# Row sums of an attention pair: written to DRAM as nine rows after one transpose, instead of element by element

## The chip, the cores and the metric

The kernel runs on one core of a Trainium2 chip. The metric is the device time of one execution in microseconds; the median of three runs of the kernel before is 1294.0 us (1293.81 to 1294.35). Engines are named as in the profile: PE (TensorE; PEld its weight loads), DVE (VectorE), ACT (ScalarE), POOL (GpSimd) and SP (SyncE), which issues every DMA of this program on one queue, in program order.

## The reference

```
q_pool = q.reshape(2, 8, 576, 2, 64).mean(axis=3)        # pairs of queries averaged
scores = q_pool @ k.T / 8 ; scores -= max(scores)         # 576 x 1152 for each of 16 heads
attn   = exp(scores); attn /= attn.sum(-1) + 1e-9
x      = (attn @ v), heads side by side                   # 1152 tokens x 512
h = x @ w_in; x = (h * tanh(softplus(h))) @ w_out         # 512 -> 2048 -> 512
P = 8 rounds of Sinkhorn on exp(x @ w_gate - max)         # 1152 x 8 gates
out = sum over 8 experts of P[:, e] * (relu(x @ w1[e]) @ w2[e])
```

All values are float32; the kernel keeps each operand as a high and a low part and multiplies them in several passes. What is changed lies in the attention, at the division by the row sums `attn.sum(-1) + 1e-9`.

## The kernel before, in words

**Attention.** Two heads form a pair (8 pairs). The 2 x 576 query rows of a pair make nine tiles of 128 rows, numbered t = 0 to 8; tile 4 holds the end of one head and the start of the other, and so needs twelve score matmuls where the others need six. The loop at L678 has one step for each tile g = 9p + t and is a software pipeline. In program order a step does:

- `loads`: what an earlier step has put off, all of it DMAs, issued on SP (L685 to L687);
- `scores(g)`: six (tile 4: twelve) matmuls into `psS` (L453), and on DVE the negated copy to `e` with the row minimum (L458);
- `transposes(g - 3)`: nine PE transposes of the exponentials `er` (L527), evacuated by ACT as `eth` (L530) and by DVE as `etl` (L533);
- `hand_over(g - 1)`: a DMA that copies `e` of the tile before to `er` (L478), to be transposed two steps later;
- attention times values, `psA` (L548), in portions set by the table `AV`, and transposes of the next keys and queries, `psk` and `psq`;
- `exps(g)`: the exponential on ACT in place in `e` (L472), which also leaves the row sums of the tile in one column of `rs`, a tile of 128 x 9.

There are three buffers of `e` and two of `er`. Queries that have been transposed are copied to the other half of the partitions by small DMAs (`swap`, L426, tiles `qT` and `qz`); tile 4 needs `qz`.

**Row sums.** When pair p - 1 is complete, in the step t = 0 of pair p, `row_sums` (L480) adds EPS, takes the reciprocal on DVE (L482, L483) and puts two things on `loads`. `out` (L488) writes the 128 x 9 reciprocals into a DRAM tile `row`, transposed by its access pattern: each element goes to its own place, 1152 elements of 4 bytes. `back` (L493), one step later, reads `row` twice, spread over 64 partitions each, into `rx`. `back` waits until `row` has landed. `rx` is used by POOL once in each pair (L571), after the last `psA` of the pair.

**After the attention.** From step g = 73 on, `mish_step` starts the first layer of the next stage (L224, `ph`), which reads `xh` and `xl`, made by POOL after L571; weights come by `raw` DMAs (L139). From there to the end PE works through that stage (L224, L767) and the experts (L1028, L1186).

Of the kernel before, what the change touches and what calls it, by code (L numbers as in the profile page):

```python
# [8 lines left out]
F32 = mybir.dt.float32  # L9
# [14 lines left out]
def pool_attention_mish_sinkhorn_kernel(  # L24
# [12 lines left out]
    nc = tc.nc  # L37
    P = 128
    B, H, S, D = q.shape
    SQ = S // 2  # L40
# [6 lines left out]
    NPAIR = B * H // 2  # L47
    HPB = H // 2
    QTL = 2 * SQ // P
# [15 lines left out]
    ident = const.tile([P, P], F32, name="ident")  # L65
# [39 lines left out]
    def run(t, eng, most=99):  # L105

        q = queue[eng]
        while q and q[0][0] <= t and most > 0:
            q.pop(0)[1]()
            most -= 1  # L110
# [180 lines left out]
    with ExitStack() as actx:  # L291
        def pool(name, bufs, **kw):
            return actx.enter_context(tc.tile_pool(name=name, bufs=bufs, **kw))
# [20 lines left out]
        rx_p = pool("rx", 1)  # L314
        row_p = pool("row", 2, space=bass.MemoryType.DRAM)
# [5 lines left out]
        for i in range(2):  # L321
            t = z_p.tile([P, 2, 2, P], F32R, name=f"qz{i}")
# [4 lines left out]
        loads = []  # L327
# [20 lines left out]
        def split_kv(p, j, which, eng, part, more=True):  # L348
            if p == NPAIR:
                return  # L350
            raw = raws[which, p, j]
            pl, dst = (kst_p, kst) if which == "k" else (vst_p, vst)
            if part == 0:
                t = dst[p, j] = pl.tile([P, NK, 2, D], F32R, tag=which + "st", name=f"{which}st{p}_{j}")
                split_hi(eng, t[:, :, 0, :], raw)
            else:
                t = dst[p, j]
                split_lo(eng, t[:, :, 1, :], raw, t[:, :, 0, :])
                p, j = (p, 1) if j == 0 else (p + 1, 0)
                if more and p < NPAIR:  # L360
                    loads.append(lambda: load_kv(p, j, which))
# [79 lines left out]
        scS, eS, erS, rsS, rxS = {}, {}, {}, {}, {}  # L441

        def scores(g, pl=None):
            p, t = divmod(g, QTL)
            ps = (pl or ps_s).tile([P, 3, 512], F32, tag="s", name=f"psS{g}")
            for kb in range(3):
                if t == MID:
                    ops = [(qz[p % 2][:, j, s, :], kT[p, j]) for j in range(2) for s in range(2)]
                else:
                    x, i = q_tile(p, t)  # L450
                    ops = [(x[:, i, s, :], kT[p, int(t > MID)]) for s in range(2)]
                for n, (a, kt) in enumerate(ops):
                    nc.tensor.matmul(  # L453
                        ps[:, kb, 0:TH], lhsT=a, rhs=kt[:, kb * TH:(kb + 1) * TH],
                        start=(n == 0), stop=(n == len(ops) - 1))
            sc = e_p.tile([P, 3, TH], F32, tag="e", name=f"e{g}")
            nm = tiny.tile([P, 1], F32, tag="nm", name=f"nm{g}")
            nc.vector.tensor_scalar(  # L458
                sc, ps[:, :, 0:TH], -1.0, None, op0=ALU.mult, op1=ALU.min, accum_out=nm)
            scS[g] = (sc, nm)  # L460

        def exps(g):
            p, t = divmod(g, QTL)
            sc, nm = scS.pop(g)
            sc = sc.rearrange("p a b -> p (a b)")
            if g < 2:
                e = erS[g] = er_p.tile([P, S], F32, tag="er", name=f"er{g}")
            else:
                e = eS[g] = sc
            if t == 0:  # L470
                rsS[p] = tiny.tile([P, QTL], F32, tag="rs", name=f"rs{p}", bufs=2)
            nc.scalar.activation(e, sc, AF.Exp, bias=nm, scale=-1.0, accum_out=rsS[p][:, t:t + 1])  # L472

        def hand_over(g):

            e = eS.pop(g)
            er = erS[g] = er_p.tile([P, S], F32R, tag="er", name=f"er{g}")
            nc.sync.dma_start(out=er.bitcast(F32), in_=e)  # L478

        def row_sums(p):  # L480
            rs = rsS.pop(p)
            nc.vector.tensor_scalar(rs, rs, EPS, None, op0=ALU.add)  # L482
            nc.vector.reciprocal(rs, rs)  # L483
            row = row_p.tile([QTL * P], F32, tag="row", name=f"row{p}")
            rx = rxS[p] = rx_p.tile([P, SQ], F32, tag="rx", name=f"rx{p}")

            def out():
                nc.sync.dma_start(out=row.rearrange("(t p) -> p t", p=P), in_=rs)  # L488
                loads.append(back)

            def back():
                for j in range(2):
                    nc.sync.dma_start(  # L493
                        out=rx[j * D:(j + 1) * D, :], in_=row[j * SQ:(j + 1) * SQ].unsqueeze(0).to_broadcast([D, SQ]))

            loads.append(out)


        c0, c1 = 2 * P, SQ
# [80 lines left out]
        def run_av(n):  # L580
            for _ in range(n):
                if av_todo:
                    av_todo.pop(0)()
# [31 lines left out]
        ps_t = bctx.enter_context(tc.tile_pool(name="ps_w", bufs=2, space=PSUM))  # L615
# [38 lines left out]
        def prep(p, t):  # L654
            for x, at_ in (PREP if p else PREP0).items():
                if at_ == t:
                    if x[0] == "q":
                        split_q(p + 1, nc.gpsimd, int(x[1]))
                    else:
                        split_kv(p + (x[0] == "k"), int(x[1]), x[0], nc.gpsimd, int(x[2]))  # L660

        def turn(p, t):
            fs = []
            for j in range(2):
                pp = p + (j == 0)
                if pp < NPAIR:
                    fs += [
                        lambda pp=pp, j=j, c=c: trans_k(pp, j, c)
                        for c in range(3) if TURN["k10" if p == 0 and j == 1 else f"k{j}"][c] == t]
            for u in range(3):  # L670
                pp = p + (u == 0)
                if p == 0 and TURN["q0"][u] == t:
                    fs.append(lambda u=u: trans_q0(u + 2))
                if 0 < pp < NPAIR and TURN["q"][u] == t:
                    fs.append(lambda pp=pp, u=u: trans_q(pp, u))
            return fs

        for g in range(T0 + EARLY):  # L678
            p, t = divmod(g, QTL)
            if g == 1:  # L680
                bctx.close()
                ps_t = pool("ps_t", 4, space=PSUM)
                ps_a = pool("ps_a", 1, space=PSUM)
            pre = turn(p, t) if g < NQ else []
            waiting, loads[:] = loads[:], []  # L685
            for f in waiting:
                f()  # L687
            if g < LAG:
                exps(g)
                for f in pre:  # L690
                    f()
                if g + 1 < LAG:
                    split_kv(0, 0, "v", nc.gpsimd, g)
                    scores(g + 2, ps_s)
            else:
                if LAG < g < NQ:
                    scores(g)
                if p and g < NQ:
                    prep(p, t)
                if g < T0:  # L700
                    run(g, "dve")
                if pre:
                    pre.pop(0)()
                spread = 0 < p < NPAIR
                if spread:
                    run_av(AV[t][0])
                ready = len(av_todo)
                if g < NQ + LAG:
                    transposes(g - LAG)
                if g <= NQ:  # L710
                    hand_over(g - 1)
                if not p:
                    prep(p, t)
                run_av(min(ready, AV[t][1] if spread else 9 if g < NQ else 18))
                for f in pre:
                    f()
                if g < NQ:
                    exps(g)
            if p and t == 0:
                row_sums(p - 1)  # L720
            if late:
                late.pop(0)()
            if g < T0:
                run_all(g)
            if g == QTL:
                load_gate()
            if g == NQ - 1:
                sctx.close()
                ps_o = ctx.enter_context(tc.tile_pool(name="ps_o", bufs=3, space=PSUM, side="right"))
                wpools["d0"] = ctx.enter_context(tc.tile_pool(name="wd0", bufs=1, side="right"))  # L730
                mctx = ExitStack()
                wpools["d1"] = mctx.enter_context(tc.tile_pool(name="wd1", bufs=1, side="right"))
                wpools["t"] = mctx.enter_context(tc.tile_pool(name="wt2", bufs=3, side="right"))
            if g >= T0:
                mish_step(g - T0)
# [546 lines left out]
```

## Time and profile before

| | us |
|---|---|
| median of three runs | 1294.0 |
| the profiled execution's own time | 1296.31 |
| its span, first to last instruction | 1294.5 |

| engine | busy, us | share of the span |
|---|---|---|
| PE | 1233.8 | 95% |
| DVE | 853.2 | 66% |
| POOL | 622.1 | 48% |
| ACT | 596.6 | 46% |

The shares are means over stages that differ. In the page's forty slices the attention is the first ten; there DVE is at six to seven tenths, ACT at five to seven, PE at seven to nine, and the DMA engines at six to eight. In the later slices PE is at nine tenths or more and the DMA engines at one or two. The clock that was granted to PE is at 0.88 in the attention after the first pair and at 1.00 in the stages that follow. A wait is read from the timeline and the table of waits: how long an engine was idle, and whose end released it.

### The profile page before, as it was taken

The page shows a single profiled execution, that of the slowest core. Times are in us where ns is not written, and L with a number is a line of the kernel's source. Part 1 is how long each engine was busy: PE and PEld are TensorE (multiplying, and loading weights), DVE is VectorE, ACT ScalarE, POOL GpSimd, SP SyncE. Part 2 cuts the span into 40 slices and gives each one's busy share as a digit, 9 for nine tenths or more (in the row PEclk, how much of TensorE's full clock was granted, in tenths as well). Part 3 has the DMA queues.
Part 4 walks back from the last instruction along what each step waited for, and adds up shares of the span by engine and source line. Part 5 has one row for each costly group of instructions (what it writes and reads, how often), then busy time and mean ns, then how long its engine had stood idle before and what let it go on. Part 6 is the DMA issues. An engine that isn't in the chain of part 4 may idle for free.

```text
span 1294.5 us, 19313 instructions
## 1 busy us (share of the span) xinstructions
PE 1233.8 (95%) x6832; PEld 1134.3 (88%) x6832; DVE 853.2 (66%) x1580; ACT 596.6 (46%) x1364; POOL 622.1 (48%) x704
## 2 busy tenths in 40 slices
PE   8889787897999999999999999999999999999999
PEld 8779777787999999999888888889989998888887
DVE  7677666776464443368786666866776666866865
ACT  7677666775665454345233333333333333333331
POOL 5345524532253433327575555555555555555552
PEclk9889888988999999999999999999999999999999
DMA  6878888866432222001011111111111111111111
GB/s 207 196 191 224 241 193 173 199 224 159 130 112 82 82 82 62 13 17 50 26 45 38 49 49 49 50 42 49 50 49 50 49 50 49 31 40 42 45 49 73
DMA packets 76751, 116.84 MB, mean 90 GB/s; under 512 B 16496, under 2 KB 49008, under 8 KB 76656
## 3 DMA queue, kind: packets, MB, share of 16 engines
q1 hardware_dynamic: 76656, 115.62, 32.3%
q8 instruction: 54, 0.88, 0.3%
q14 instruction: 41, 0.34, 0.1%
HBM read 66.86 MB, written 2.40 MB: 54 GB/s over the span
## 4 chain that ended last, share of the span: by engine, by line
PE 81%; DMA 10%; DVE 6%; ACT 2%; issue 1%; SPq 1%; POOL 0%; ACTq 0%; DVEq 0%; POOLq 0%
PE po L1186 29%; PE c L1028 24%; PE ph L224 8%; PE po L767 7%; DMA er<-e 7%; PE psS L453 5%; DVE e L458 3%; PE psA L548 2%; DVE etl L533 2%; PE psT L527 1%; DMA qz<-qz 1%; DMA raw<-in_moe_w_in_dram 1%; DMA row<-rs 1%; ACT eth L530 1%; DVE xs L562 0%
## 5 line engine op out<-in xcount | busy, mean ns | idle before, releaser
L81 POOL TENSOR_TENSOR wslotsl<-s,wslotsh 128x256 fp32r<-128x256 f32 x180 | 132.3, 743 | 238.3 <-ACT wslotsh L74 227.2
L1194 DVE SCALAR_TENSOR_TENSOR oacc<-po,Pm,oacc 128x512 f32<-128x512 f32 (+1 forms) x217 | 161.2, 747 | 102.8 <-PE po L1186 95.4
L1186 PE MATMUL po<-wdbl,hhall 128*128 128x512 f32 (+1 forms) x543 | 214.6, 395 | 0.0
L1186 PE MATMUL po<-wdbh,hlall 128*128 128x512 f32 (+1 forms) x543 | 214.2, 395 | 0.0
L1186 PE MATMUL po<-wdbh,hhall 128*128 128x512 f32 (+1 forms) x543 | 214.2, 394 | 0.0
L458 DVE TENSOR_SCALAR_CACHE_REDUCE e<-psS 128x1152 f32<-128x1152 f32 x72 | 97.4, 1353 | 91.1 <-PE psS L453 46.0
L1045 ACT ACTIVATE t<-c 128x384 f32<-128x384 f32 x80 | 39.2, 490 | 247.1 <-PE c L1028 247.1
L1065 ACT ACTIVATE hhall<-c 128x384 fp32r<-128x384 f32 x180 | 88.5, 492 | 129.0 <-DVE c L1061 126.3
L1186 PEld LDWEIGHTS po<-wdbh,hhall 128*128 128x128 f32 x543 | 102.1, 188 | 24.3
L1186 PEld LDWEIGHTS po<-wdbl,hhall 128*128 128x128 f32 x543 | 102.1, 188 | 23.3
L1186 PEld LDWEIGHTS po<-wdbh,hlall 128*128 128x128 f32 x543 | 102.1, 188 | 23.2
L530 ACT ACTIVATE eth<-psT 128x384 fp32r<-128x384 f32 (+1 forms) x240 | 92.6, 477 | 57.1 <-PE psT L527 56.6
L81 POOL TENSOR_TENSOR wslotsl<-rawu,wslotsh 128x256 fp32r<-128x256 f32 x120 | 91.6, 777 | 51.5 <-ACT wslotsh L74 51.5
L533 DVE TENSOR_TENSOR etl<-psT,eth 128x384 fp32r<-128x384 f32 (+1 forms) x240 | 108.2, 508 | 5.6 <-ACT eth L530 4.4
L1066 DVE SCALAR_TENSOR_TENSOR hlall<-c,hhall 128x384 fp32r<-128x384 f32 x180 | 98.9, 549 | 2.1
L527 PE MATMUL psT<-identr,er 128*128 128x128 f32 x630 | 69.4, 256 | 32.3 <-DMA er<-e 31.0
L548 PE MATMUL psA<-etl,vst 128*128 128x256 f32 (+1 forms) x288 | 88.9, 326 | 9.0 <-DVE xs L562 8.5
L527 PEld LDWEIGHTS psT<-identr,er 128*128 128x128 f32 x630 | 63.4, 145 | 37.3 <-issue 32.9
L1028 PE MATMUL c<-x2h,wslotsl 128*128 128x384 f32 x280 | 94.8, 339 | 0.0
L1028 PE MATMUL c<-x2h,wslotsh 128*128 128x384 f32 x280 | 94.5, 338 | 0.0
L1028 PE MATMUL c<-x2l,wslotsh 128*128 128x384 f32 x280 | 94.2, 336 | 0.0
L472 ACT ACTIVATE e<-e,nm 128x1152 f32<-128x1152 f32 x70 | 89.0, 1271 | 0.9 <-ACT eth L530 0.8
(355 smaller groups left out, 3108.5 us busy)
## 6 DMA issues: line engine op xcount, KB each, us to landing
er<-e SPq DMA_DIRECT2D x70, 576.0 KB, 4.1
rawd<-in_moe_w_dram SPq DMA_DIRECT2D x60, 256.0 KB, 2.7
rawu<-in_moe_w_dram SPq DMA_DIRECT2D x30, 384.0 KB, 3.2
raw<-in_moe_w_in_dram SPq DMA_DIRECT2D x16, 512.0 KB, 3.9
raw<-in_moe_w_out_dram SPq DMA_DIRECT2D x16, 512.0 KB, 3.7
vraw<-in_v_dram SPq DMA_DIRECT2D x16, 288.0 KB, 3.9
kraw<-in_k_dram SPq DMA_DIRECT2D x15, 288.0 KB, 4.2
qraw<-in_q_dram SPq DMA_DIRECT2D x7, 576.0 KB, 6.8
```

Of the source, the lines that this page charges most:

```text
L81: eng.tensor_tensor(out=lo, in0=src, in1=hi.bitcast(F32), op=ALU.subtract)
L224: nc.tensor.matmul(ps[:, 0:TH], lhsT=a, rhs=b, start=(n == 0), stop=(n == len(ops) - 1))
L458: nc.vector.tensor_scalar(sc, ps[:, :, 0:TH], -1.0, None, op0=ALU.mult, op1=ALU.min, accum_out=nm)
L527: nc.tensor.transpose(pt[:, i, :], e[:, c * P:(c + 1) * P], ident if g < 2 else identr)
L530: nc.scalar.activation(eh[:, cs, o:o + b - a], ps[:, 0:3, a:b], AF.Copy)
L533: nc.vector.tensor_tensor(out=el[:, cs, o:o + b - a], in0=ps[:, 0:3, a:b], in1=eh[:, cs, o:o + b - a].bitcast(F32), op=ALU.subtract)
L548: nc.tensor.matmul(box["ps"][:, 0:n], lhsT=vst[p, j][:, c].rearrange("p a d -> p (a d)"), rhs=(el, eh)[which][:, c, 0:n], start=(c == 0 an ...
L767: nc.tensor.matmul(ps[:, 0:TH], lhsT=a, rhs=b, start=(n == 0), stop=(n == len(ops) - 1))
L1028: nc.tensor.matmul(cb[c], lhsT=a_, rhs=b_, start=FIRST[n] and m == 0, stop=LAST[n] and m == len(ops) - 1, skip_group_check=True)
L1066: los.append(lambda: nc.vector.scalar_tensor_tensor(out=lo, in0=b, scalar=0.0, in1=hi.bitcast(F32), op0=ALU.max, op1=ALU.subtract))
L1186: nc.tensor.matmul(ps[:, 0:w], lhsT=a, rhs=b[:, cs], start=(n == 0), stop=(n == len(ops) - 1))
L1194: nc.vector.scalar_tensor_tensor(out=oa, in0=ps[:, 0:w], scalar=gate, in1=oa, op0=ALU.mult, op1=ALU.add)
```

## The change

`row_sums` keeps the addition and the reciprocal. A new function, `turn_sums`, is called one step later (t = 1). It turns the 128 x 9 reciprocals into 9 x 128 by one PE transpose into a PSUM tile of the pool that `psT`, `psk` and `psq` use, copies them on DVE to an SBUF tile `rt`, and puts the write on `loads`. The DRAM tile `row` is now 9 x 128, and each of its rows is written from one partition of `rt` as 512 contiguous bytes. For all pairs but the last the write is put off by one step more, so that it is issued at the start of step t = 3 and the reads into `rx` at the start of t = 4; for the last pair they are issued at the start of the second and third step after the pair's end.

```
         def row_sums(p):
-            rs = rsS.pop(p)
+            rs = rsS[p]
             nc.vector.tensor_scalar(rs, rs, EPS, None, op0=ALU.add)
             nc.vector.reciprocal(rs, rs)
-            row = row_p.tile([QTL * P], F32, tag="row", name=f"row{p}")
+
+        def turn_sums(p):
+
+            ps = ps_t.tile([P, 4, P], F32, tag="t", name=f"psr{p}")
+            nc.tensor.transpose(ps[0:QTL, 0, :], rsS.pop(p), ident)
+            rt = rx_p.tile([QTL, P], F32, tag="rt", name=f"rt{p}")
+            nc.vector.tensor_copy(rt, ps[0:QTL, 0, :])
+            row = row_p.tile([QTL, P], F32, tag="row", name=f"row{p}")
             rx = rxS[p] = rx_p.tile([P, SQ], F32, tag="rx", name=f"rx{p}")
 
             def out():
-                nc.sync.dma_start(out=row.rearrange("(t p) -> p t", p=P), in_=rs)
+                nc.sync.dma_start(out=row, in_=rt)
                 loads.append(back)
 
             def back():
+                flat = row.rearrange("t p -> (t p)")
                 for j in range(2):
                     nc.sync.dma_start(
-                        out=rx[j * D:(j + 1) * D, :], in_=row[j * SQ:(j + 1) * SQ].unsqueeze(0).to_broadcast([D, SQ]))
-
-            loads.append(out)
+                        out=rx[j * D:(j + 1) * D, :], in_=flat[j * SQ:(j + 1) * SQ].unsqueeze(0).to_broadcast([D, SQ]))
+
+            loads.append(out if p == NPAIR - 1 else lambda: loads.append(out))
...
             if p and t == 0:
                 row_sums(p - 1)
+            if p and t == 1:
+                turn_sums(p - 1)
```

On SP, around the end of the third pair, the order before is this (`er` are the hand-overs, `qT` and `qz` the swapped queries, `vraw` and `raw` loads from DRAM):

```order
L478 DMA er_1619<-e_1551 128x1152
L488 DMA row_1637<-rs_1133 128x9x1
L478 DMA er_1683<-e_1596 128x1152
L493 DMA rx_1638<-row_1637 64x576 x2
L426 DMA qT_1_1655<-qT_1_1655 64x4x128 x2
L426 DMA qz_137<-qz_137 64x2x128 x2
L478 DMA er_1738<-e_1647 128x1152
L337 DMA vraw_1_1753<-in_v_dram 128x576
```

The same place of the changed kernel:

```order
L478 DMA er_1627<-e_1559 128x1152
L478 DMA er_1688<-e_1604 128x1152
L426 DMA qT_1_1660<-qT_1_1660 64x4x128 x2
L426 DMA qz_137<-qz_137 64x2x128 x2
L478 DMA er_1747<-e_1652 128x1152
L495 DMA row_1704<-rt_1702 9x128
L337 DMA vraw_1_1763<-in_v_dram 128x576
L426 DMA qT_2_1758<-qT_2_1758 64x128 x2
L478 DMA er_1812<-e_1717 128x1152
L139 DMA raw_0_2_1828<-in_moe_w_in_dram 128x512
L501 DMA rx_1705<-row_1704 64x576 x2
L478 DMA er_1868<-e_1774 128x1152
```

The write has moved behind one more hand-over and the swaps, and four other entries (five DMAs) now stand between it and the reads, where one hand-over stood.

On DVE at the same place the changed kernel has this order (`wt` are pieces of the weight preparation):

```order
L483 RECIPROCAL rs_1137<-rs_1137 128x9
L458 TENSOR_SCALAR e_1652,nm_1653<-psS_1645 128x1152
L162 SCALAR_TENSOR_TENSOR wt_0_1_1607<-raw_0_1_1324,wt_0_1_1607 128x256
L541 TENSOR_TENSOR etl_3_1669<-psT_0_1670,eth_3_1668 128x3x128
L541 TENSOR_TENSOR etl_3_1669<-psT_1_1676,eth_3_1668 128x3x128
L541 TENSOR_TENSOR etl_3_1669<-psT_2_1682,eth_3_1668 128x3x128
L490 COPY rt_1702<-psr_1700 9x128
L458 TENSOR_SCALAR e_1717,nm_1718<-psS_1710 128x1152
```

The copy L490 is the only new instruction there; it stands between the last `etl` of one step and the score copy of the next. On PE the transpose L488 stands at the same place, between the last `psA` of step t = 1 and the six `psS` matmuls of t = 2.

At the end of the last pair the order on SP before is:

```order
L139 DMA raw_0_2_4078<-in_moe_w_out_dram 128x512
L488 DMA row_4076<-rs_3620 128x9x1
L493 DMA rx_4077<-row_4076 64x576 x2
L139 DMA raw_1_0_4177<-in_moe_w_in_dram 128x512
L139 DMA raw_0_3_4179<-in_moe_w_out_dram 128x512
```

In the changed kernel it is:

```order
L139 DMA raw_0_2_4104<-in_moe_w_out_dram 128x512
L495 DMA row_4152<-rt_4150 9x128
L139 DMA raw_1_0_4207<-in_moe_w_in_dram 128x512
L139 DMA raw_0_3_4209<-in_moe_w_out_dram 128x512
L501 DMA rx_4153<-row_4152 64x576 x2
```

Two weight loads have moved ahead of the reads into `rx`.

## Rows read from the trace of the kernel before

**Rows 1.** The page's chain that ended last, by line.

```profile
PE po L1186 29%; PE c L1028 24%; PE ph L224 8%; PE po L767 7%; DMA er<-e 7%; PE psS L453 5%; DVE e L458 3%; PE psA L548 2%; DVE etl L533 2%; PE psT L527 1%; DMA qz<-qz 1%; DMA raw<-in_moe_w_in_dram 1%; DMA row<-rs 1%; ACT eth L530 1%; DVE xs L562 0%
```

**Rows 2.** Busy time by stage: the attention from its second pair; the passage after it.

```profile
core 0: us, PE busy (x) PEld busy (x) DVE busy (x) ACT busy (x) POOL busy (x), PEclk, DMA share, GB/s
...
38.00:328.50 290.50, 240.04 (x1665) 225.04 (x1664) 198.05 (x404) 200.24 (x448) 120.54 (x117) 0.88 0.78 199
328.50:359.00 30.50, 28.54 (x173) 27.60 (x174) 13.94 (x26) 18.85 (x39) 8.16 (x7) 1.00 0.40 114
```

**Rows 3.** Timeline of SP: start, duration of the issue, line, tiles.

```profile
121.52 0.39 SPq L488 DMA_DIRECT2D row<-rs  x1
122.07 0.49 SPq L478 DMA_DIRECT2D er<-e  x1
133.40 1.12 SPq L493 DMA_DIRECT2D rx<-row  x2
...
136.00 1.24 SPq L426 DMA_DIRECT2D qz<-qz  x2
137.33 0.56 SPq L478 DMA_DIRECT2D er<-e  x1
```

**Rows 4.** DMA issues of the whole span: count, KB each, median us to landing.

```profile
er<-e SPq DMA_DIRECT2D x70, 576.0 KB, 4.1
...
qraw<-in_q_dram SPq DMA_DIRECT2D x7, 576.0 KB, 6.8
...
out_dram<-oacc SPq DMA_DIRECT2D x2, 128.0 KB, 1.7
row<-rs SPq DMA_DIRECT2D x8, 4.5 KB, 10.1
```

**Rows 5.** DMA traffic from 121 to 134 us.

```profile
DMA packets 1319, 0.62 MB, mean 48 GB/s; under 512 B 1185, under 2 KB 1185, under 8 KB 1319
...
er<-e SPq DMA_DIRECT2D x1, 576.0 KB, 11.9
```

**Rows 6.** Waits of the DMA queue: total us, times, longest.

```profile
SPq L493 <- DMA row<-rs: 74.1, 8, 10.8
```

**Rows 7.** Timeline of DVE and PE, same place: start, duration, [idle before <- releaser].

```profile
124.39 1.35 DVE L458 TENSOR_SCALAR_CACHE_REDUCE e<-psS 128x1152 f32<-128x1152 f32 x1
...
134.04 1.36 DVE L458 TENSOR_SCALAR_CACHE_REDUCE e<-psS 128x1152 f32<-128x1152 f32 x1 [6.69 <-DMA er<-e]
134.06 1.35 PE L527 MATMUL psT<-identr,er 128*128 128x128 f32 x9 [5.70 <-DMA er<-e]
...
141.46 1.36 DVE L458 TENSOR_SCALAR_CACHE_REDUCE e<-psS 128x1152 f32<-128x1152 f32 x1 [3.69 <-PE psS L453]
```

**Rows 8.** Seven windows, L458 of tile 2 to L458 of tile 4, summed.

```profile
sum 124.00, PE 79.62 PEld 72.78 DVE 45.90 ACT 49.42 POOL 32.79; mean PE 11.37 PEld 10.40 DVE 6.56 ACT 7.06 POOL 4.68
```

**Rows 9.** Six windows, L458 of tile 4 to L458 of the next tile 2, summed.

```profile
sum 144.70, PE 139.82 PEld 132.76 DVE 132.04 ACT 131.72 POOL 82.82; mean PE 23.30 PEld 22.13 DVE 22.01 ACT 21.95 POOL 13.80
```

**Rows 10.** Busy time just after the wait of rows 7, and later in that pair.

```profile
134.00:138.50 4.50, 3.54 (x20) 3.38 (x20) 3.68 (x7) 1.25 (x3) 0.00 (x0) 0.50 0.58 153
138.50:145.00 6.50, 6.31 (x41) 5.74 (x41) 3.23 (x6) 4.80 (x9) 0.67 (x1) 0.91 0.90 272
145.00:154.00 9.00, 8.09 (x69) 7.59 (x69) 6.23 (x12) 7.42 (x16) 7.30 (x7) 1.00 1.02 350
```

**Rows 11.** Pieces of the chain of waits: start, us, what.

```profile
119.31 1.04 PE psS L453 x6
...
328.58 9.45 DMA row<-rs
```

**Rows 12.** The dearest like operations: a float32 PE transpose; a DVE read of PSUM.

```profile
L527 PE MATMUL psT<-ident,er x18: 272/273/331, 15.4 to 20.0; 128*128 128x128 f32 x18
...
L533 DVE TENSOR_TENSOR etl<-psT,eth 128x384 fp32r<-128x384 f32 (+1 forms) x240 | 108.2, 508 | 5.6 <-ACT eth L530 4.4
```

**Rows 13.** Timeline of PE after the attention: the longest wait there.

```profile
348.14 0.45 PE L224 MATMUL ph<-xl,wuh 128*128 128x384 f32 x1 [1.06 <-POOL xl L81]
```

## What is predicted, and how it is worked out

> **What bounds the kernel now.** I read the chain of waits first [rows 1]. Most of it is PE work of the later stages, which this change doesn't touch. What is not PE work and stands high is the hand-over DMA `er<-e`, 7% of the span, in a kernel whose hand-overs are meant to be hidden by the two steps between copy and use. The busy times by stage say where to look: from 38 to 328.5 us, in which 63 tiles run, PE is idle for 290.5 - 240.0 = 50.5 us, and its granted clock is 0.88; in the passage behind it PE is idle for 2.0 us at a clock of 1.00 [rows 2]. So a gain can come from those 290.5 us, and hardly from elsewhere.
>
> Next the queue's own timeline, around one pair's end [rows 3]. The element-wise `row` write is issued at 121.52, the next hand-over 0.55 us later, and then SP issues nothing until 133.40, when `row` has landed and the reads into `rx` may go. Everything behind them in the queue is late by that much: the swaps of `qz` go out at 136.00, the following hand-over at 137.33. In total SP stands at this wait for 74.1 us in eight pairs [rows 6]. The hand-over just behind the write is slow too: it lands 11.9 us after its issue, against a median of 4.1 us; in that stretch the DMA engines moved 1319 packets, 1185 of them under 512 bytes, and 1152 of these are the elements of `row` [rows 4, 5].
>
> The engines feel both halves [rows 7]. DVE copies the scores of tile 2 at 124.39; for tile 3 it waits 6.69 us for the hand-over to free its buffer, and PE waits 5.70 us to transpose the same tile; tile 4 then comes only at 141.46, since `qz` and the next hand-over were issued late. After the wait PE runs for a while at a granted clock of 0.50, the lower of its two levels (1.2 GHz), and is back at 1.00 only later in the pair [rows 10].
>
> **What the two late tiles are worth.** I cut the pairs at the score copies. From tile 2 to tile 4, two intervals, seven times: 124.0 us together, 17.7 each, with DVE busy for 6.6, ACT for 7.1 and PE for 11.4 of it, PE partly at the low clock [rows 8]. From tile 4 to the next pair's tile 2, seven intervals, six times: 144.7 us, or 144.7 / 42 = 3.45 per tile, with PE busy for 139.8, and DVE and ACT for 132 (91%) [rows 9]. That is the pace of this pipeline when no `row` write is in its way, near the limit of three engines. If tiles 3 and 4 ran at it, they would take 2 x 3.45, and 1.04 more for the six extra matmuls of tile 4 [rows 11], in all 7.93. Seven times 7.93 is 55.5. The most that the change can return here is therefore 124.0 - 55.5 = 68.5 us. At pair 3 the parts would be 6.2 of 9.65 us in the first interval and 2.9 of 7.42 in the second [rows 7].
>
> **The change, part by part.**
>
> Removed: the 1152 elements in each pair, so that the hand-over no longer waits behind them, and the wait of SP between write and reads. Gain as above, 68.5. What is late next in place of the 11.9 us hand-over is PE itself: with the hand-over landing 4.1 us after 122.07, at 126.2, PE would reach its transposes with the data there.
>
> Added: eight PE transposes of 9 x 128 and eight DVE copies. Neither shape is in the trace. A float32 transpose of 128 x 128 takes 0.27 us, a DVE read of three times as many columns from PSUM 0.51, so a third of it, 0.17, is my estimate for the copy [rows 12]. Below nothing neither can go. Two engines at 91% and 97% cover no such work, so I count both in full. The PSUM tile also shifts which of the four buffers the following transposes get, by one; the next `psT` then waits for the copy rather than for an older reader, some tenths at most. I take 0.5 us in each of seven pairs for all of it (0.2 to 0.9), 3.5 us. The copy holds up only the score copy behind it in DVE's queue.
>
> Moved: the write goes behind two hand-overs and two pairs of swaps, the reads behind one more hand-over, a pair of swaps and two loads. SP's own time for issues doesn't change, 0.4 to 0.6 us for each DMA. POOL's use of `rx` comes after the last `psA` of the pair, in step 5, more than one step behind the reads in either order.
>
> Crowding: today the loads and hand-overs held up by `row` go out together and fill the DMA engines, 350 GB/s at a share of 1.02 [rows 10]. From 134 to 154 us 5.6 MB moved (4.5 x 153, 6.5 x 272, 9 x 350), 16 us at that rate. With the wait gone the same tiles start at 125 and end some 9 us earlier, which leaves 20 us. So the engines are enough, but a hand-over may meet queries and weights. It has 6.9 us (two tiles) from issue to use and needs 4.1; the worst median of its size is 6.8 [rows 4]. I take 1.2 us lost in each pair, half as much again as PE's idle time in the good stretches (4.9 / 6 = 0.8), with bounds of 0 and 2.7 (6.8 - 4.1): 8.4 us.
>
> After the last pair the chain goes through the `row` write for 9.45 us [rows 11]. PE had other work beside it, and waits at most 1.06 us, for `xl` [rows 13]. `row` is issued one step later than now but lands faster, and two weight loads go ahead of the reads; I take 1.0 us of gain (0 to 1.4).
>
> **Sum.** 68.5 - 3.5 - 8.4 + 1.0 = 57.6 us. The profiled execution took 1296.3, 1.8 more than its span and 2.3 more than the median of the runs. It would become 1238.7, and the median 1294.0 - 57.6 = 1236.4, so I forecast 1236. With every bound on the good side the gain is 68.5 - 1.4 + 1.4 = 68.5, 1225.5; with every one on the bad side 68.5 - 6.3 - 18.9 = 43.3, 1250.7.
>
> **Rivals.**
>
> *The wait moves to the reads.* They still wait for `row`, and the hand-over of tile 3 is behind them. The nine rows may land in 1.7 us, as the small stores to DRAM at the end do, or, if they queue behind the hand-over issued just before, in up to 4.1 + 1.7 = 5.8 [rows 4]. SP comes to the reads about one tile, 3.45 us, later, so it stands there for 0 to 2.4 us. In the sum this is nothing, since the hand-over has 2.8 us to spare; if crowding has used that up, it is 2.4 us in seven pairs, 17 us: 1253. The Trainium skill (DMA: Bandwidth & Descriptors, Queues, rings and completion order) says that each DMA engine takes the descriptors of a ring in order. The trace agrees: the hand-over behind the elements took 11.9 us [rows 5]. By that rule the new write can't overtake the hand-over ahead of it, which is the upper end here.
>
> *Tile 4 still waits.* `qz` comes by two swaps that now follow the hand-over and may land too late. Then only the first interval is mended, and pair 3's 2.9 us stays in seven pairs: 20 us, 1257. Against it: behind the hand-over of 122.07 and one other pair of swaps (1.24 us a pair) they would be issued at about 124 instead of 136.00 [rows 3], and tile 4's matmuls are due at 124.39 + 7.93 - 2 x 1.04 = 130.2.
>
> *The write is as slow as before.* If nine rows of 512 bytes from nine partitions take as long as the elements, the order alone is changed. The time then lies at no gain and the new work, 1294.0 + 3.5 = 1297. The packets counted [rows 5] speak against it, since nine take the place of 1152.
>
> *Slower.* One mechanism: the write lands so late that SP is held at the reads for longer than now, with hand-over, queries and keys behind it. SP is held for 74.1 / 8 = 9.3 us today [rows 6]; with 3.45 us between the two this begins at a landing of 12.7 us. The element-wise write took 133.40 - 121.52 = 11.9 us beside a hand-over [rows 3]. At 15 us it would cost 2.3 us in seven pairs and the new work: 1294.0 + 16 + 3.5 = 1314. Nothing in the trace suggests it for nine packets.
>
> **Chances.** Forecast, with its own range of 1225 to 1251: 0.74. A wait moved to the reads: 0.10. Tile 4 still late: 0.09. Faster than 1225, because the long stretches also gain from free DMA engines: 0.03. Write as slow as before: 0.02. Slower by the held queue: 0.02. The range that should hold the time 8 times in 10 is 1224 to 1254; it takes in the first rival. A measurement of this kernel tells 0.2%, 2.6 us, from no change. Faster: 0.74 + 0.10 + 0.09 + 0.03 = 0.96; the same 0.01; slower 0.03, the last two cases shared.
>
> **What would show it.** In the changed profile the two-tile stretches should take about 9 us instead of 17.7, the seven-tile ones still about 24; the clock of the attention should be near 1.00; no hand-over should take more than about 7 us; SP's wait for `row` should be under 2.4 us in a pair; packets under 512 bytes should fall by some 9200; the time from the end of the attention to the end of the program should be as now. I am wrong if PE or DVE still waits for hand-overs in tiles 3 and 4, if tile 4 waits for `qz`, or if the long stretches grow by what the short ones lose.

## The result and the profile after

The changed kernel takes 1234.83 us (median of 4 runs, 1234.14 to 1235.62), the kernel before in the same runs 1294.17. The ratio is 0.954, with a 95% interval of 0.9524 to 0.9557. The forecast was 1236, the range 1224 to 1254. The profiled execution took 1235.16 us, with a span of 1233.3: 61.2 less than before. By the medians the gain is 59.3, where 57.6 was forecast.

The first view is the chain that ended last, by line, as in [rows 1]:

```profile
PE po L1196 30%; PE c L1038 26%; PE ph L224 10%; PE po L777 8%; PE psS L453 5%; PE psA L556 5%; DVE e L458 3%; PE psT L535 2%; DVE etl L541 2%; DVE xs L570 1%; ACT e L472 1%; ACT eth L538 1%; PE psk L391 1%; PE pg L832 0%; ACT kT L392 0%
```

The hand-over `er<-e`, 7% before, is gone from it, and so are `qz` and `row`. What has grown is attention times values: `psA` from 2% to 5%, and its evacuation, `DVE xs`, from 0 to 1%.

The stages as in [rows 2]: the window, its length, then each engine's busy time, the clock, the DMA share and GB/s:

```profile
37.80:273.00 235.20, 219.31 (x1691) 208.66 (x1690) 201.30 (x411) 201.45 (x450) 121.59 (x117) 1.00 0.74 247
273.00:303.00 30.00, 29.88 (x182) 29.52 (x181) 18.87 (x30) 23.55 (x48) 13.49 (x10) 1.00 0.42 121
```

The same 63 tiles take 235.2 us, not 290.5. PE was idle for 50.5 us and is now for 235.2 - 219.3 = 15.9; its busy time fell by 20.7, because the clock rose from 0.88 to 1.00. Both changes come out of the same waits: in [rows 10] the low clock stands right behind the wait, and in e2 below it moves with the stall.

The two sums of windows that the forecast rests on, as in [rows 8] and [rows 9], seven stretches from tile 2 to tile 4 first:

```profile
sum 66.30, PE 56.28 PEld 54.14 DVE 47.29 ACT 49.21 POOL 34.41; mean PE 8.04 PEld 7.73 DVE 6.76 ACT 7.03 POOL 4.92
...
sum 143.90, PE 139.34 PEld 132.15 DVE 132.65 ACT 132.19 POOL 80.95; mean PE 23.22 PEld 22.03 DVE 22.11 ACT 22.03 POOL 13.49
```

Here is where the time came from: 124.0 - 66.3 = 57.7 us from tiles 3 and 4, and 0.8 from all the others. From the last pair's row sums (the start of DVE L482) to the end the program ran 966.4 us before and runs 963.9 now, 2.5 less; the start gave 0.3. Together 61.3, against 61.2 measured.

The waits that were to vanish, total us, times and longest. DVE's wait for the hand-over [rows 7], before and then after, and SP's wait for `row` [rows 6]:

```profile
DVE e L458 <- DMA er<-e: 44.4, 13, 6.7
...
DVE e L458 <- DMA er<-e: 4.6, 5, 1.2
...
SPq L501 <- DMA row<-rt: 1.0, 1, 1.0
```

SP waited 74.1 us for `row` and now waits 1.0, DVE for the hand-over 44.4 us in 13 waits and now 4.6 in 5. The issues with their median landing, as in [rows 4], and the packets:

```profile
DMA packets 67551, 116.84 MB, mean 95 GB/s; under 512 B 7224, under 2 KB 39808, under 8 KB 67456
...
er<-e SPq DMA_DIRECT2D x70, 576.0 KB, 3.6
```

The longest landing of a hand-over is 6.0 us, where it was 11.9. Packets under 512 bytes fell by 9272. The two new instructions, with shortest, median and longest ns:

```profile
L488 PE MATMUL psr<-ident,rs x8: 271/271/271, 39.7 to 272.3; 128*9 128x128 f32 x8
L490 DVE COPY rt<-psr x8: 269/269/278, 40.9 to 273.5; 9x128 f32<-9x128 f32 x8
```

The queue in the same pair as [rows 3] never stands for longer than 2.8 us between two issues. The write stands behind two hand-overs that stood behind it before; the section on the change counted only one:

```profile
105.10 1.50 SPq L426 DMA_DIRECT2D qT<-qT  x2
106.66 1.36 SPq L426 DMA_DIRECT2D qz<-qz  x2
108.58 0.50 SPq L478 DMA_DIRECT2D er<-e  x1
109.18 0.45 SPq L495 DMA_DIRECT2D row<-rt  x1
...
112.30 0.48 SPq L478 DMA_DIRECT2D er<-e  x1
...
113.50 1.49 SPq L501 DMA_DIRECT2D rx<-row  x2
```

And DVE and PE there, to be read against [rows 7]:

```profile
107.19 1.33 DVE L458 TENSOR_SCALAR_CACHE_REDUCE e<-psS 128x1152 f32<-128x1152 f32 x1
...
110.97 1.36 DVE L458 TENSOR_SCALAR_CACHE_REDUCE e<-psS 128x1152 f32<-128x1152 f32 x1 [0.83 <-PE psS L453]
...
112.99 0.48 DVE L570 TENSOR_TENSOR xs<-psA,avt 64x320 f32<-64x320 f32 x1
...
113.53 0.39 PE L556 MATMUL psA<-etl,vst 128*128 128x256 f32 x1 [1.30 <-DVE xs L570]
...
114.67 2.32 PE L453 MATMUL psS<-kT,qz 128*128 128x384 f32 x12
...
117.03 1.36 DVE L458 TENSOR_SCALAR_CACHE_REDUCE e<-psS 128x1152 f32<-128x1152 f32 x1 [2.03 <-PE psS L453]
```

Tile 3, the second of these copies, no longer waits for the hand-over that frees its buffer: it comes 3.78 us after tile 2, at 107.19, against 9.65 before. But tile 4 comes 117.03 - 110.97 = 6.06 us later, where the forecast had 3.45 + 1.04 = 4.49 before its allowance. No DMA is named there. PE waits 1.30 us at L556, because `psA` has one buffer and DVE has yet to evacuate it into `xs`; the last `psA` portion of step t = 3 stands in PE's queue ahead of tile 4's twelve score matmuls, so these are late, and DVE idles 2.03 us for them. The table of waits of the kernel before had this wait already; before and after:

```profile
PE psA L548 <- DVE xs L562: 8.5, 14, 1.2
...
PE psA L556 <- DVE xs L570: 10.0, 14, 1.3
```

### The profile page after: what moved, and what is told of

Its sections match the earlier page's. It is cut to its first block, busy times and chain, and to the rows that moved or that the text cites. A ratio compares the mean times of both kernels' runs of the same rounds, so it can differ in the third digit from the quotient of the medians.

```text
span 1233.3 us, 19334 instructions
## 1 busy us (share of the span) xinstructions
PE 1209.1 (98%) x6840; PEld 1114.4 (90%) x6840; DVE 854.4 (69%) x1588; ACT 596.9 (48%) x1364; POOL 623.7 (51%) x704
## 4 chain that ended last, share of the span: by engine, by line
PE 89%; DVE 7%; ACT 2%; issue 1%; DMA 0%; SPq 0%; POOL 0%; ACTq 0%; DVEq 0%
PE po L1196 30%; PE c L1038 26%; PE ph L224 10%; PE po L777 8%; PE psS L453 5%; PE psA L556 5%; DVE e L458 3%; PE psT L535 2%; DVE etl L541 2%; DVE xs L570 1%; ACT e L472 1%; ACT eth L538 1%; PE psk L391 1%; PE pg L832 0%; ACT kT L392 0%
## 5 line engine op out<-in xcount | busy, mean ns | idle before, releaser
L458 DVE TENSOR_SCALAR_CACHE_REDUCE e<-psS 128x1152 f32<-128x1152 f32 x72 | 97.2, 1351 | 30.2 <-PE psS L453 24.3
L556 PE MATMUL psA<-etl,vst 128*128 128x256 f32 (+1 forms) x288 | 83.4, 311 | 10.5 <-DVE xs L570 10.0
L453 PE MATMUL psS<-kT,qT 128*128 128x384 f32 x384 | 82.1, 348 | 4.9 <-DVE e L458 4.7
L74 ACT ACTIVATE wslotsh<-s 128x256 fp32r<-128x256 f32 x180 | 72.0, 411 | 24.3 <-DVE s L1004 24.3
```

What stands on the lines that cost most here:

```text
L453: nc.tensor.matmul(ps[:, kb, 0:TH], lhsT=a, rhs=kt[:, kb * TH:(kb + 1) * TH], start=(n == 0), stop=(n == len(ops) - 1))
L458: nc.vector.tensor_scalar(sc, ps[:, :, 0:TH], -1.0, None, op0=ALU.mult, op1=ALU.min, accum_out=nm)
L556: nc.tensor.matmul(box["ps"][:, 0:n], lhsT=vst[p, j][:, c].rearrange("p a d -> p (a d)"), rhs=(el, eh)[which][:, c, 0:n], start=(c == 0 an ...
```

## Experiments

The theory on trial: the elements of `row` make the DMA engines slow, and SP's wait for `row` holds up the queue, two costs that add. The rivals: one of them is all of it; the number of packets is not what costs; tile 4's late start is DMA crowding. Runs e and f were made on one chip, g on another; each is compared with the kernel before on its own chip by the ratio. The kernel before took 1294.2 us in the first runs, 1288.2 to 1288.9 on the chip of e and f, and 1286.7 on that of g, and its only profile is of the first runs. So a window sum of a variant of it that lies some 6 us below [rows 8] shows no gain. The changed kernel took 1234.8 and 1235.7 us in the two places where it ran, and its sums agree (66.30 and 143.90, in g0 66.10 and 143.70).

**e1: only the reads later.** The kernel before, with the two reads put off by two more steps, so that SP doesn't wait for `row` at them:

```diff
-                loads.append(back)
+                loads.append(back if p == NPAIR - 1 else lambda: loads.append(lambda: loads.append(back)))
```

> The kernel before, with the element-wise write where it was and only the reads into rx put off to step t = 4, so that SP issues swaps and hand-overs without waiting. Theory of the packets (1152 elements hold up whatever stands behind them on the DMA engines): the hand-over behind the write still lands 11 to 12 us after its issue and tile 3 still waits about 6 us; only what the late issue of qz and of the next hand-over cost in tile 4 comes back, some 4 us in each of seven pairs: about 1266 us. Rival, the wait of SP in its queue is the whole cost: 1240 us or less. Rival, the packets are the whole cost: 1285 us or more.

Measured: 1285.47 against 1288.86, ratio 0.9973 (0.9962 to 0.9984). The first theory's gain did not come; the figure is that of the last rival, but the run doesn't prove it, since the queue stopped elsewhere. From the chain of waits, the queue's waits, the timeline of SP, and the two-tile windows:

```profile
120.02 11.23 DMA er<-e
```

```profile
SPq L426 <- DMA row<-rs: 26.3, 5, 6.1
...
SPq L337 <- DMA row<-rs: 6.2, 1, 6.2
```

```profile
124.21 0.58 SPq L337 DMA_DIRECT2D vraw<-in_v_dram  x1
130.57 1.16 SPq L426 DMA_DIRECT2D qT<-qT  x2
```

```profile
sum 117.40, PE 76.21 PEld 71.93 DVE 45.83 ACT 50.05 POOL 34.70; mean PE 10.89 PEld 10.28 DVE 6.55 ACT 7.15 POOL 4.96
```

The hand-over behind the write is as slow as ever, so tile 3 still waits. And SP stopped again, 32.5 us in six waits, at a swap or a load that doesn't read `row`; in the timeline above it is the eighth DMA after the write. In the trace the DMAs report their landing on eight semaphores (counters that tell that a piece of work is done), one after the other in the order of issue, so the eighth comes round to the one that `row` still holds. (The reads of the last pair weren't put off, and wait 8.9 us.) The swaps of `qz` landed 10.3 us after their issue, by the median. So putting off the reads alone is worth 0.3%; what the queue's wait would be worth if it vanished altogether, this run doesn't show.

**e2: only the elements.** The changed kernel's order, but no transpose and no copy; `row` is written element by element as before:

```diff
...
-                nc.sync.dma_start(out=row, in_=rt)
+                nc.sync.dma_start(out=row.rearrange("t p -> p t"), in_=rs)
```

> The changed kernel's order of DMAs, but the row sums are written element by element from the untransposed tile (no transpose, no copy). Theory of the packets: the hand-over issued after the write in step t = 3 lands some 11 us later, and SP stands at the reads for 7 to 8 us with the next hand-over behind it, so the stall moves from tiles 3 and 4 to tiles 5 and 6 and nearly all of the gain is lost: 1275 to 1295 us. Rival, the new order alone makes the gain because one more step lies between write and reads: under 1250 us.

Measured: 1284.88 against 1288.86, ratio 0.9966 (0.9952 to 0.998). The two sums of windows, two tiles and then seven:

```profile
sum 68.60, PE 56.75 PEld 54.14 DVE 47.20 ACT 49.65 POOL 30.45; mean PE 8.11 PEld 7.73 DVE 6.74 ACT 7.09 POOL 4.35
...
sum 182.20, PE 153.08 PEld 144.04 DVE 131.77 ACT 132.33 POOL 84.77; mean PE 25.51 PEld 24.01 DVE 21.96 ACT 22.05 POOL 14.13
```

The two-tile stretches are mended, and the long ones have grown by 38.3 us; PE is busy in them for 153.1 us, where the changed kernel has 139.3 for the same work at the full clock. The chain shows the elements in their new place: SP waits at the reads until they have landed, and issues the next hand-over only then:

```profile
122.97 12.66 DMA row<-rs
...
136.90 6.21 DMA er<-e
```

The delay goes where the elements go. Of the 4.0 to 4.6% that the change is worth, nearly all hangs on how `row` is written, not on when.

**e3: not put off.** The changed kernel with the write issued one step earlier, right behind the copy:

```diff
-            loads.append(out if p == NPAIR - 1 else lambda: loads.append(out))
+            loads.append(out)
```

> The changed kernel without the additional step before the write: row is issued at the start of t = 2 and read at the start of t = 3, for every pair. Theory (nine rows land within a step, whatever the step): the time stays that of the changed kernel within 3 us, 1232 to 1238. Rival (the reads would have waited, the putting off is what hides the write): SP waits 1 to 2.4 us at the reads in each pair and the time is 5 to 17 us longer, 1240 to 1252.

Measured: 1234.12 against 1288.86, ratio 0.9572 (0.9549 to 0.9594), within 2 us of the changed kernel in its own runs. SP waits a little more for `row`, and it costs nothing:

```profile
SPq L501 <- DMA row<-rt: 4.3, 7, 1.0
```

So putting the write off isn't needed. The nine rows in the old place exactly, at t = 0, were not tried.

**e4: tile 4's wait.** The changed kernel with the last seven `psA` matmuls of step t = 3 moved behind the score matmuls of t = 4 (each entry of `AV` gives the portions before and after the transposes of a step):

```diff
-        AV = [(0, 9), (0, 8), (0, 8), (2, 7), (0, 4), (7, 4), ...
+        AV = [(0, 9), (0, 8), (0, 8), (2, 0), (7, 4), (7, 4), ...
```

> The changed kernel with one number moved in the table AV: the seven psA matmuls of the last group, which stand in step t = 3 and wait 1.3 us for DVE to empty the one psA buffer, stand after the scores of t = 4 instead. Theory (tile 4 comes 1.6 us later than the good pace because these seven wait in PE's queue ahead of its twelve score matmuls, and not because of any DMA): the stretch from tile 2 to tile 4 falls from 9.5 to about 7.5 us; what of it stays gained depends on the stretch behind, where the seven matmuls (0.8 us) must now run: 1222 to 1232 us. Rival (tile 4 is late because of qz or of a hand-over): the stretch stays at 9.5 us and the time at 1234 to 1237.

Measured: 1224.33 (1222.03 to 1224.67) against 1288.86, ratio 0.949 (0.9463 to 0.9518). The two sums:

```profile
sum 51.90, PE 49.98 PEld 48.95 DVE 46.67 ACT 46.25 POOL 32.52; mean PE 7.14 PEld 6.99 DVE 6.67 ACT 6.61 POOL 4.65
...
sum 147.20, PE 142.33 PEld 136.16 DVE 132.87 ACT 132.88 POOL 82.98; mean PE 23.72 PEld 22.69 DVE 22.15 ACT 22.15 POOL 13.83
```

The two-tile stretches lose 14.4 us, the others grow by 3.3. Of the 14.4, 6.3 is PE work that has moved out of these stretches; the rest, 8.1, is idle time of PE. PE's wait at `psA`, 10.0 us in the changed kernel, has gone with it:

```profile
PE psA L556 <- DVE xs L570: 1.9, 7, 0.5
```

What was left over tile 4 was the wait for the one buffer of `psA`. This is the fastest version of the study, 9.8 us under e3 on the same chip.

**f4: the same edit on the kernel before.**

> The kernel before with the same edit of the table AV that took 10 us off the changed kernel (seven psA matmuls moved behind the scores of tile 4). Theory (before the change tile 4 waits for qz and for hand-overs, and the wait for the psA buffer lies inside that wait): nothing, ratio 0.997 to 1.003. Rival (the two waits add up): ratio 0.992.

Measured: 1292.11 against 1288.22, ratio 1.0031 (1.0017 to 1.0045). The time doesn't fall. (The two-tile sum is 118.4; that it lies 5.6 us below [rows 8] is no more than the 5.9 us by which the two chips differ.) PE's wait at `psA` has gone, and in its place PE waits for `qz`, 22.9 us, where it waited 6.9 in the kernel before:

```profile
PE psS L453 <- DMA qz<-qz: 22.9, 7, 4.5
...
PE psA L548 <- DVE xs L562: 2.0, 7, 0.5
```

The gain of e4 exists only since the change: before, the buffer's wait lay inside a longer one.

**f1: half the elements.** The kernel before; `row` holds 576 elements, and both reads take these:

```diff
-                nc.sync.dma_start(out=row.rearrange("(t p) -> p t", p=P), in_=rs)
+                nc.sync.dma_start(out=row.rearrange("(t p) -> p t", p=D), in_=rs[0:D, :])
...
```

> The kernel before, in its own order, but only the row sums of 64 of the 128 rows of each tile are written (576 elements, not 1152) and both halves of rx read those: it leaves out half of the row sums. Theory of the packets (each element takes its time on the 16 engines, so the hold-up is proportional): the hand-over behind the write lands about 7 us after its issue instead of 11 to 12, SP's wait for row falls from about 10 to about 6 us, and since a hand-over has 2.8 us to spare, some 60 to 75% of the gain of the change is there: ratio to the kernel before 0.965 to 0.975. Rival (a fixed cost of element-wise writes or of the wait itself): 0.99 or more.

Measured: 1285.64 against 1288.22, ratio 0.9984 (0.9974 to 0.9993). Half the elements don't give half the gain. The write's landing, the hand-over in the chain, and SP's wait:

```profile
row<-rs SPq DMA_DIRECT2D x8, 2.2 KB, 8.6
```

```profile
118.96 8.58 DMA er<-e
```

```profile
SPq L493 <- DMA row<-rs: 60.8, 8, 9.0
```

The hold-up is shorter, but not half: the hand-overs behind the seven writes land in 7.8 to 10.1 us (median 8.6), in the kernel before in 9.1 to 11.9 (median 10.8). Tile 3 comes 5.8 to 8.1 us after tile 2, before 6.9 to 9.7, and tile 4 8.3 to 10.6 after tile 3, before 7.4 to 10.9; part of that can be the difference of the chips. The doubt this raised about the number of packets led to the g runs.

**f2: another queue.** e1 with the write issued by ACT, so that the hand-over isn't behind it in SP's queue:

```diff
-                nc.sync.dma_start(out=row.rearrange("(t p) -> p t", p=P), in_=rs)
+                nc.scalar.dma_start(out=row.rearrange("(t p) -> p t", p=P), in_=rs)
```

> The kernel before with the element-wise write issued from ACT's DMA queue at the same step, and the reads on SP put off to step t = 4. Theory A (what hurts is the order inside one ring: the hand-over stands behind the elements): on another queue's ring it interleaves with them, lands in 5 to 8 us, and most of the gain is there, ratio 0.955 to 0.970 (ACT pays 0.5 us an issue). Theory B (the elements hold the 16 engines themselves, whatever the ring): the hand-over still lands 10 us or more after its issue, ratio 0.985 or more.

Measured: 1285.34 against 1288.22, ratio 0.9975 (0.9964 to 0.9986). The chain, and the issues:

```profile
120.39 11.65 DMA er<-e
```

```profile
qz<-qz SPq DMA_DIRECT2D x14, 64.0 KB, 10.6
...
row<-rs ACTq DMA_DIRECT2D x8, 4.5 KB, 10.6
```

A hand-over from another queue is as slow, and one that was issued 0.2 us ahead of the write took 12.4 us. It isn't the order within one queue.

**f3: nothing at all.** The changed kernel with `rx` set to ones once; transpose, copy, write and reads are gone:

```diff
+        rx_one = rx_p.tile([P, SQ], F32, tag="rx", name="rx_one")
+        nc.gpsimd.memset(rx_one, 1.0)
...
-            ps = ps_t.tile([P, 4, P], F32, tag="t", name=f"psr{p}")
...
+            rsS.pop(p)
+            rxS[p] = rx_one
+            return
```

> The changed kernel without the way of the row sums through DRAM: rx is set to ones once, so the division by the row sums is left out, and with it the transposes, the copies, the write and the reads. It shows what the way still costs. Theory (as in the sum: 0.5 us of new work in a pair, everything else hidden): 3 to 4 us less than the changed kernel, about 1231. Rival (the new work is covered, and so are the DMAs): within 1.5 us of the changed kernel. Rival (reads and write still hold up hand-overs): 8 us less or more.

Measured: 1232.37 against 1288.22, ratio 0.957 (0.9555 to 0.9584); on that chip e3 took 1234.12, and its profile's span is 1230.0, against 1232.4 for e3 and 1233.3 for the changed kernel in the first runs. So all that is left of the row's way costs some 1.8 to 3.3 us. The seven-tile windows:

```profile
sum 140.70, PE 137.14 PEld 131.13 DVE 130.36 ACT 130.20 POOL 81.10; mean PE 22.86 PEld 21.85 DVE 21.73 ACT 21.70 POOL 13.52
```

They are 3.2 us shorter than the changed kernel's; the two-tile sums are equal (66.3).

**g0 to g3: what in the elements costs.** The changed kernel again (g0), and three kernels that add to it one spare write of the 1152 row sums in each of seven pairs, issued at t = 1, which nobody reads. They differ in where the elements go: in g1 packed, as before; in g2 each at the start of its own 512 bytes; in g3 the nine of a partition side by side, 128 stores of 36 bytes.

```diff
+                scr = row_p.tile([QTL * P], F32, tag="scr", name=f"scr{p}")
+                loads.append(lambda: nc.sync.dma_start(out=scr.rearrange("(t p) -> p t", p=P), in_=rs))
# g2 in their place:
+                scr = row_p.tile([QTL * P, P], F32, tag="scr", name=f"scr{p}")
+                loads.append(lambda: nc.sync.dma_start(out=scr.rearrange("(t p) x -> p t x", p=P)[:, :, 0], in_=rs))
# g3:
+                scr = row_p.tile([P, QTL], F32, tag="scr", name=f"scr{p}")
+                loads.append(lambda: nc.sync.dma_start(out=scr, in_=rs))
```

> The changed kernel itself, on the chip of the runs beside it: ratio to the kernel before 0.954 to 0.958.

> The changed kernel with one DMA more in each of seven pairs: the old element-wise write, at its old place in step t = 1, to a DRAM tile that nobody reads. It has the price of the elements without any wait for them. Theory (what passes the DMA engines behind the elements is slowed until their stores are done, some 10 us): hand-over and qz are late as in the kernel before, 1275 to 1290 us. Rival (it needs the reader's wait in SP's queue as well): under 1250 us.

> As the run with the spare elements, but each of the 1152 elements goes to its own 512 bytes of DRAM, and not next to 127 others. Theory C (the stores are slow since many engines write into the same few lines of DRAM; the packets themselves pass in 1 us): the hold-up goes away, under 1250 us. Theory D (a store of 4 bytes is slow wherever it goes, or the number of stores counts): as with neighbouring elements, 1275 to 1290 us.

> As the run with the spare elements, but each partition's nine values go side by side as one store of 36 bytes, 128 stores in place of 1152 (the data in another order; nobody reads them). Theory D (number of stores): a ninth of the hold-up, about 1 us, which a hand-over has to spare: 1235 to 1242 us. Theory C (shared lines): 128 stores from 16 engines still share lines, so more than a ninth: 1245 to 1275 us.

Measured, with 1286.72 for the kernel before: g0 1235.70 (ratio 0.960, 0.9584 to 0.9616), g1 1275.83 (0.9914, 0.9896 to 0.9933), g2 1235.63 (0.9603, 0.9589 to 0.9617), g3 1235.94 (0.9598, 0.9584 to 0.9612). The spare write's issues with their median landing, of g1, g2 and g3:

```profile
scr<-rs SPq DMA_DIRECT2D x7, 4.5 KB, 10.8
```

```profile
scr<-rs SPq DMA_DIRECT2D x7, 4.5 KB, 2.6
```

```profile
scr<-rs SPq DMA_DIRECT2D x7, 4.5 KB, 1.7
```

g1 and g2 have the same number of packets under 512 bytes, 15400 each, and the same elements from the same queue in the same place of the program. One costs 40.1 us, the other nothing. The cost lies in the two-tile stretches, of g1 and then of g0:

```profile
sum 108.80, PE 75.65 PEld 71.73 DVE 45.70 ACT 48.64 POOL 34.69; mean PE 10.81 PEld 10.25 DVE 6.53 ACT 6.95 POOL 4.96
...
sum 66.10, PE 55.95 PEld 53.81 DVE 46.99 ACT 49.13 POOL 34.76; mean PE 7.99 PEld 7.69 DVE 6.71 ACT 7.02 POOL 4.97
```

Nobody reads the spare elements, but they are not quite without a wait: SP stops six times at the eighth DMA after them, as in e1:

```profile
SPq L337 <- DMA scr<-rs: 22.0, 6, 5.4
```

On this chip the kernel before took 1286.7 us, so g1 has 40.1 of the 51.0 us between it and the changed kernel. What the DMA engines moved in the 13 us from the write's issue, in forty slices of 0.325 us, of g1 and then of g2:

```profile
GB/s 28 14 15 7 7 369 425 340 0 0 0 14 57 99 57 0 0 57 128 43 0 0 28 0 57 85 28 46 22 32 101 216 238 270 229 236 227 269 261 280
```

```profile
GB/s 14 28 15 7 7 369 411 354 454 260 202 139 276 295 167 99 0 326 425 383 454 227 170 227 405 232 88 2 213 440 440 383 298 93 164 290 378 302 350 337
```

For eight slices they are alike: the write and the first 0.37 MB of the hand-over go by. Then g1's engines move 34 GB/s on average for 22 slices, 7 us, which is about the rest of the hand-over, while g2's go on. In this time a packet of 4608 bytes, a piece of the hand-over, takes 2.0 us by the median; before it, and in g2, it takes 0.18. The packets of the elements take 7 ns each in both runs and have passed within the first eight slices. What makes the engines slow is therefore not the passing of 1152 small packets but where they are stored. g3's stores are neighbours too and cost nothing; it changes their number and their size at once, so which of the two spares it the hold-up isn't shown.

## Why the prediction held, point by point

**The stall of tiles 3 and 4: right, as to place and size.** It named two-tile stretches of about 9 us: 66.3 / 7 = 9.5. The long ones stayed at 24 (143.9 / 6), the clock went to 1.00, no hand-over stands in the way, SP's wait is 1.0 us once, the longest landing of a hand-over is 6.0 us, and packets under 512 bytes fell by 9272 for the 9200 named. Its figure of 68.5 as the most that could return here, less crowding and new work, was 56.6; 57.7 came. One reading was off: the tile that PE waits 5.70 us to transpose [rows 7] is not tile 3 but tile 0 of the pair, whose hand-over it is.

**Two halves: both from one cause, and unequal.** The prediction spoke of engines that feel both halves, the slow DMA and the held queue, and gave neither a price of its own. Later reads alone gave 0.3% (e1), the whole new order with elements also 0.3% (e2), and the mended write 4.3% with less putting off (e3). The held queue is a consequence of the late `row`, beside a slow hand-over that holds the same tiles. The elements without a reader have 40.1 of 51.0 us (g1). What the wait at the reads adds to that is by estimate some 10 us: the 10.9 that are left, more by the new work, less by the gain after the last pair. No run has the slow elements without any stop of the queue.

**New work, 3.5 us: right within its bounds.** f3 puts it at 1.8 to 3.3 by time and span, with what is left of the DMAs. The copy takes 0.27 us, where the estimate was 0.17, the transpose 0.27. f3's windows put it in the seven-tile stretches; these still shrank by 0.8, and without it by 4.0. Whether free DMA engines gave them that, as the 3% case had it, isn't shown: in e1, with the elements, the same windows sum to 141.9.

**Crowding, 8.4 us: near in size, wrong in cause, and so luck.** This is the step that failed. Against 55.5 at full pace the two-tile stretches are 10.8 us too long, and the missing time is at tile 4. The hand-overs aren't crowded: their median fell from 4.1 to 3.6, and DVE waits for them 1.2 us at most. It is the single buffer of `psA`, shown by e4, which took 8.1 us of PE's idle time out of these stretches with the DMA as it was. The table of waits before had it, 8.5 us in 14 waits, but no term of the sum did. It cost nothing then (f4); what the prediction left out is what would hold tile 4 once the hand-over no longer did.

**After the last pair, 1.0 us: too small in this pair of profiles.** 2.5 came, over the bound of 1.4. The reads of the last `row` are issued 5.7 us after the row sums, where they took 10.0 before; so POOL's multiplication starts 12.0 us after the row sums and not 16.2:

```profile
269.41 0.15 DVE L482 TENSOR_SCALAR rs<-rs 128x9 f32<-128x9 f32 x1
...
275.10 1.12 SPq L501 DMA_DIRECT2D rx<-row  x2
...
281.43 1.54 POOL L579 TENSOR_TENSOR xs<-xs,rx 128x576 f32<-128x576 f32 x1 [20.30 <-DVE wdl L81]
```

The bound came from one PE wait of 1.06 us [rows 13]. Two more waits of PE stood beside it, 0.5 us for `hlall` and 0.4 for `xh`, and all three are gone, 2.0 us together; the other 0.5 is not followed. The size isn't firm: the same stretch takes 963.8 to 964.0 us in six of the seven profiles with nine rows and 966.6 in g2, and 964.9 to 967.9 in the five with all elements.

**The rivals.** The reads hardly wait (1.0 us once), tile 4's `qz` is on time (no wait for it is left), and the queue isn't held. "The write is as slow as before" was set aside because nine packets take the place of 1152. The conclusion was right, the reason isn't: g2's 1152 packets cost nothing. Nor does the rule that was cited for a ring's order explain the 11.9 us hand-over [rows 5]: f2 puts the write into another queue, and the hand-over still takes 11.65. What was drawn from it for the new write fits: issued 0.6 to 1.2 us behind a hand-over it lands in 2.7 to 4.2 us, within the 5.8 allowed, and in e3, where the last hand-over was issued 3.5 us earlier, in 1.8 to 2.4.

## What to carry to other kernels

Look in the trace for a DMA of scattered 4-byte stores, and price it by what lands late behind it, on any queue, not by its own bytes or its number of packets alone. When a queue's wait and a slow transfer hold up the same tile, neither is worth its own time: mend the one that causes the other; here the milder mends gave 0.3%. And after a large wait has gone, read the next limit in the same tiles before sharing the blame out to DMA crowding; here it was one accumulation buffer, worth another 10 us, and its wait already stood in the table before.

## What the runs showed of the hardware that was not expected

Two things. First, 1152 stores of 4 bytes to neighbouring addresses in DRAM take 10.8 us to land and hold up what the DMA engines do for some 7 us, also for another queue (11.65 us for a hand-over, f2); half as many still take 8.6; the same stores 512 bytes apart land in 2.6 us and hold up nothing, and 128 neighbouring stores of 36 bytes land in 1.7. The Trainium skill (DMA: Bandwidth & Descriptors, Specifications) says that below 512 bytes the DMA reads, modifies and writes. If stores to one stretch of memory must then follow one another, packed elements would be slow and spread ones not, as g1 and g2 are; but no run here shows that step, and neither the distance nor the number at which the cost begins was looked for. Second, a wait that was taken away in the queue's order came back at the eighth DMA behind the write, through a shared completion semaphore: 32.5 us over six waits in e1, and 22.0 over six in g1.
